# Running the 64-row products of a fused attention, gated and low-rank kernel over all 128 rows

## The chip, the cores and the metric

The kernel runs on one core of one Trainium2 chip. The metric is device time in microseconds (us) of the whole kernel. Engines: PE is TensorE's matrix products (PEld its weight loads), DVE is VectorE, ACT is ScalarE, POOL is GpSimd, SP is SyncE, which issues the transfers.

## What is computed

Three blocks follow each other: attention with rotary positions (4 batches, 8 heads, 576 tokens, 64 features per head), a gated block with a product over the tokens ("spatial mix"), and a block with a rank-32 product over the tokens followed by a two-layer channel block.

```
scores = (1/8) * q_rot @ k_rot.T;  attn = exp(scores - max) / (sum + 1e-9);  x = attn @ v      # per head
h = gelu(x @ w_in);  u, v = halves of h;  v_n = layernorm(v) * g_ln
x = x + (u * (w_sg @ v_n + b_sg)) @ w_out                   # w_sg is 576 x 576, over tokens
x = x + ((x.T @ U) @ V).T                                   # U is 576 x 32, V is 32 x 576
out = x + relu(x @ w_ch1) @ w_ch2
```

## The kernel before, in words

Products run in the type F32R (`float32r`), which keeps only part of a float32. To keep precision, an operand is split into a high part (a copy in that type) and a low part (what is left), and a product of two split operands is the sum of high x high, high x low and low x high. Tokens come in chunks of 128; 576 is four chunks and a tail of 64 (`TS`, L91). For a tail, one tile of 128 partitions holds the high part in its upper 64 partitions and the low part in its lower 64, so that one product over 128 rows does two of the three: the other operand then has its high part in both halves. The third product is the one that this change is about.

Attention (L119 to L465). The work runs in ticks, one for each chunk of a head's scores, 5 per head, 32 heads, in an order that is written out by hand on all engines (L424 to L458). In a tick `scores` makes one chunk of scores in PSUM (four products, L248), ScalarE takes the exponential, and for the first chunk and the tail (`SPLITS`, L136) it makes the high part `ph` (L257) and VectorE the low part (L263). `row_max` works ten chunks ahead: two products (L220) and VectorE's maximum (L225). Both use the three buffers "ss" of PSUM. `values`, three ticks behind, multiplies the probabilities with the values (L284) into two accumulators: an unsplit chunk takes four instructions in plain float32, the first chunk six products, and the tail, last, four. For the tail `VS` holds the high part of the values (index 0) and the low part (index 1); the 64 rows of the values stand twice in it, in both halves of the partitions. `finish` then copies the result to X (ACT, L299) and the sums of the exponentials to `sr` (DVE, L300); only after that may the next head's products into the two accumulators begin. Beside this, `later` puts steps at fixed ticks: rotary turns on POOL, and on ACT, DVE and POOL the conversion of one float64 chunk every ten ticks from tick 12 on (`converted`, with three longer DVE passes L74 to L76): eight chunks of w_in, one of U and two of V. Those of V write the high part `VH4` and the low part `VL2` (L352).

Gated block and low-rank product (L468 to L669). `v_step`, `u_step`, `s_step` (spatial mix), `o_step`, `y_step`, `z_step` and `h_step` (low-rank product with V) make products by `mm3` (L535), four PSUM tiles in turn; TensorE's order is written out (L753 to L843), that of the other engines is a scheduler's. `s_step` runs four times for each of 4 batches: twelve pairs of products for four chunks (L610), then the tail (L612) against the high part `WSH` and, over 64 rows, against the low part `WSL`. `h_step` runs four times per batch: `Z` holds its high part above and its low part below, against `VH4`, and then its upper half against `VL2`.

The channel block (L672 to L746) has no products of 64 rows.

The two lines for the tail of the probabilities and the low-rank product are:

```
280  pr = [(VS[:, 0, j], ph[:, ns]), (VS[:kk, 1, j], ph[:kk, ns])]      # kk = 64
668  mm3(ps, [(Z[:, ds_], VH4), (Z[0:64, ds_], VL2)], 2)
```

Of the kernel before, what the change touches and what calls it, by code (L numbers as in the profile page):

```python
# [17 lines left out]

# The high words of float64's 2**-127 and of the largest float32, read as float32.
F64_LEAST = 2.0**-15  # L20
# [5 lines left out]

# The chunks of keys whose probabilities are split for the product with the values.
SPLIT = slice(0, 5, 4)

# The attention runs in ticks, one for each tile of a head's scores. The other work is put between them:  # L30
# the steps that prepare a head's operands (three of rope, high parts, low parts, the row of -1), so many
# ticks before its first tile; for heads 2, 3 and 4, the ticks themselves; for heads 0 and 1, of the two
# steps of first_stacks.
LEAD = 23, 22, 19, 19, 15, 10
LEAD_IN = (-20, -19, -19, -8, -8, 1), (-19, -18, -16, -3, -1, 4), (-3, -3, 0, 2, 4, 8)
FIRST = (-17, -10), (-9, -9)
# The heads prepared without DMAs: which of their copies ScalarE makes.
BY_ACT = (0, 1, 1, 1, 1), (1, 1, 0, 1, 1), (1, 0, 1, 1, 1)
# Loads ahead of a head and of a pair's values, and the two steps of splitting the values.
LOAD, LOAD_FIRST, LOAD_V, SPLIT_V, SPLIT_V_FIRST = 30, -19, 16, (6, 1), (-11, -1)  # L40
# The maxima of rows: tiles ahead of the scores, the tick where that begins and its tiles in ten ticks,
# the tick for head 1's, and the ticks from a head's last tile of them until they are made a row.
AHEAD, RAMP_FROM, RAMP, MAX_1, ROW, ROW_0, ROW_1 = 10, -1, 25, -1, 2, -8, -9
# The steps of the sums' inverses, after a pair of heads.
INVERSE = 3, 4, 14
# The float64 matrices: first tick, ticks apart, ticks from load to arithmetic; and the split of the first rows.
MATRIX, APART, CONVERT, ROWS = 12, 10, 5, (151, 159)
# Idle products that keep TensorE's clock up until the pipeline is full: before the maxima of head 0, their
# row, the five tiles of maxima of head 1, and the first tiles of scores.
IDLE = 17, 2, 5, 0, 2, 5, 6, 1, 0, 1  # L50
# [3 lines left out]
def tile_kernel(ctx: ExitStack, tc: tile.TileContext, qk, vv, tabs, w_in, g_ln, wsgT, b_sg, w_out, u_r, v_r, w1, w2, out):  # L54
    nc = tc.nc

    def f(ap):
        return ap.bitcast(F32)
# [4 lines left out]
    def bits(ap):  # L63
        """The words of float64 rows, low and high by turns."""
        return ap.bitcast(U32)

    def from_f64(t, raw):
        """The steps of t = float32 of the float64 words in raw [p, n, 2]; too small a magnitude becomes 0."""
        lo, hi = raw[:, :, 0], raw[:, :, 1]
        tu = t.bitcast(U32)  # L70
        return (
            lambda: nc.scalar.activation(t, hi.bitcast(F32), AF.Abs),
            lambda: nc.vector.tensor_scalar(t, t, F64_LEAST, F64_MOST, ALU.max, ALU.min),  # L73
            lambda: nc.vector.tensor_scalar(tu, tu, 5, 2, ALU.logical_shift_left, ALU.logical_shift_right),  # L74
            lambda: nc.vector.scalar_tensor_tensor(tu, hi, 0xC0000000, tu, ALU.bitwise_and, ALU.bitwise_or),
            lambda: nc.vector.scalar_tensor_tensor(tu, lo, 29, tu, ALU.logical_shift_right, ALU.bitwise_or),  # L76
        )
# [21 lines left out]
    def staged(pool, src, tag="raw64", bufs=2):  # L99
        """float32 of the float64 words at src."""  # L100
        raw = pool.tile([P, 512, 2], U32, tag=tag, name=tag, bufs=bufs)
        t = pool.tile([P, 512], F32, tag="t64", name="t64", bufs=1 if tag == "raw64" else 2)
        nc.sync.dma_start(raw.rearrange("p n w -> p (n w)"), src)
        for fn in from_f64(t, raw):
            fn()
        return t

    keep = ctx.enter_context(tc.tile_pool(name="keep", bufs=1))
    # Halves of w_in, and later the first weights of the channel block.
    SETA = [keep.tile([P, KT, 512], F32R, name=f"setA{i}") for i in range(4)]  # L110
# [4 lines left out]
    VH4 = keep.tile([P, S], F32R, name="VH4")  # L115
    VL2 = keep.tile([64, S], F32R, name="VL2")

# [1 line left out]
    es1 = ExitStack()  # L119
# [28 lines left out]
    def rope(e, h):  # L148
        """The steps of turning a head's keys and queries, on engine e."""
        raw = RAW[h % NR]  # L150
        return (
            lambda: e.tensor_tensor(raw[:, 0], raw[:, 0], tab[:, 0], ALU.mult),
            lambda: e.tensor_tensor(raw[:, 1], raw[:, 1], tab[:, 1], ALU.mult),
            lambda: e.tensor_tensor(raw[:, 0], raw[:, 0], raw[:, 1], ALU.add),
        )

    def stacks(h, ticks):
        """Operands of the scores, of keys and queries in the halves of the partitions: K1 the
        keys' high parts twice, Q1 the queries' high and low parts, K2 the keys' low parts and -1,
        Q2 the queries' high parts and, later, the rows' maxima."""  # L160
        rot = RAW[h % NR][:, 0]
# [26 lines left out]
    def first_stacks(h):  # L188
        """The same without a wait for DMAs, in two parts."""
        rot = RAW[h % NR][:, 0]  # L190
# [23 lines left out]
    def row_max(h, t, done):  # L214
        """The maxima of a tile of head h's rows; and as a row, those that head `done` has."""
        ps = psp.tile([P, 2, 512], F32, tag="ss", name=f"sm{h}_{t}", bufs=3)
# [14 lines left out]
    def first_row():  # L231
        """Head 0's maxima as a row, without a DMA."""
        ps = psp.tile([P, 2, 512], F32, tag="ss", name="first_row", bufs=3)
# [31 lines left out]
    def values(h, c, t0):  # L265
# [4 lines left out]
        for n in range(2):  # L270
            ns = slice(n * HALF, (n + 1) * HALF)
            o = PVS[h][n][:, :HALF]
            if c in SPLITS:
# [3 lines left out]
                if kk == P:  # L277
                    pr = [(VS[:, 0, j], ph[:, ns]), (VS[:, 1, j], ph[:, ns]), (VS[:, 0, j], pl[:, ns])]
                else:
                    pr = [(VS[:, 0, j], ph[:, ns]), (VS[:kk, 1, j], ph[:kk, ns])]  # L280
            else:
# [41 lines left out]
    def converted(t0, src, n, use):  # L323
        """float32 of the n float64 columns at src, for the steps use(t)."""
        raw = p1.tile([P, 512, 2], U32, tag="raw64", name="raw64", bufs=1)[:, :n]
# [22 lines left out]
    def v_chunk(t0, a):  # L348
        hs = slice(a * HALF, (a + 1) * HALF)
        converted(t0, v_r[:, 2 * a * HALF:2 * (a + 1) * HALF], HALF, lambda t: (  # L350
            lambda: nc.scalar.activation(VH4[:, hs], t, AF.Copy),
            lambda: nc.gpsimd.tensor_tensor(VL2[:, hs], t[:D], f(VH4[:D, hs]), ALU.subtract),  # L352
        ))
# [59 lines left out]
    def warm(i):  # L413
        """Products of no use that keep the tensor engine's clock up."""
        if i == 0:
# [8 lines left out]
    for t in range(T0, NC * NH + LAG):  # L424
# [32 lines left out]
        for fn in due.pop(t, []):  # L457
            fn()  # L458
    # The last pair's last two steps come with the next block.
    while len(due) > 2:  # L460
# [6 lines left out]

# [1 line left out]
    es2 = ExitStack()  # L469
# [49 lines left out]
    def gelu2(dst, ps, w, pp):  # L519
        """2 * gelu_tanh(ps), in dst if there is one."""  # L520
        t = p2.tile([P, 2, 512], F32, tag="gt", name="gt", bufs=3)
# [24 lines left out]
    def x_tail(b):  # L546
        """The tails of the tokens of two batches."""
        for a in range(2):
# [7 lines left out]
    def v_step(b, t):  # L556
        """Normed rows of the tile t of tokens, at the end of a group of tiles; the tails of two batches are one tile."""
        if t == NC - 1 and b % 2:
# [46 lines left out]
    def s_step(b, d):  # L605
# [5 lines left out]
        tail = VT[:, ds_] if b % 2 else VH[:, NC - 1, ds_]  # L611
        pr += [(tail, WSH[:, NC - 1]), (tail[:D], WSL[:D, NC - 1])]  # L612
        mm3(ps, pr, 2)
# [19 lines left out]
    def y_step(b, s):  # L633
        """Rows of one or two tiles of tokens."""
        pp, nt = TS[s], min(2, NC - s)
# [28 lines left out]
    def h_step(b, d):  # L664
        Z = ZS[b]
        ps = ps_tile(f"q{b}_{d}")
        ds_ = slice(d * P, (d + 1) * P)
        mm3(ps, [(Z[:, ds_], VH4), (Z[0:64, ds_], VL2)], 2)
        nc.vector.tensor_tensor(h2(X[b][:, d]), ps[:, :, :HALF], h2(X[b][:, d]), ALU.add)  # L669

# [1 line left out]
    FG = 512  # L672
# [9 lines left out]
    def weights(pool, g, tiles):  # L682
        """The steps of loading a group's weights."""
        W[g] = tiles
# [7 lines left out]
    def spans(blk):  # L692
        """The pieces of a block of tokens that lie in one batch."""
        first = t = sum(WIDE[:blk])
# [15 lines left out]
    def c1(g, blk, i):  # L710
        """The hidden features of two tiles for a block of tokens."""
        if i == 0:
# [17 lines left out]
    def c2(g, blk, i, n=2):  # L730
        """The tiles n * i ... of output features for a block of tokens, of a group of hidden ones."""
        RH, RL = RS[g, blk]
# [14 lines left out]

# [1 line left out]
    def run(fn, b, *which):  # L749
# [153 lines left out]
```

## Time and profile before

| | us |
|---|---|
| median of 3 runs | 1003.77 |
| lowest, highest of the runs | 1003.36, 1005.98 |
| span of the profiled execution | 1002.3 |

The profiled execution's own time is given by its span, from its first to its last instruction. The page and the answers of the trace that follow are of that execution. PE is modelled: a product's busy time overlaps with its neighbours', so the pace of products is read from stretches of the chain (time by number of products) and not from a mean. In the chain, a line such as "PE pv L284 x8" stands for eight products in a row; "issue" is time in which an engine waited for nothing that the profile shows.

| stretch, us | what runs |
|---|---|
| 0 to 37 | loads, first head's operands |
| 37 to 335 | attention, 16 pairs of heads |
| 335 to 424 | gated block of batch 0 |
| 424 to 616 | low-rank product and gated block by turns, four batches |
| 616 to 1002 | channel block |

### The profile page before, as it was taken

The numbers are of one execution on the slowest core, as the hardware profiler recorded it, in microseconds if no ns is written. First come the engines' busy times: TensorE is split into PE (matmuls) and PEld (weight loads), VectorE is DVE, ScalarE is ACT, GpSimd is POOL, SyncE is SP. The second block draws the span as 40 slices with busy tenths as digits, with TensorE's granted clock in tenths as the row PEclk, the third lists the DMA queues.
The fourth block names the chain that finished last, engine by engine and source line by source line (L and its number), as shares of the span: only waits on it lengthen the run. The fifth ranks groups of instructions, "written<-read, shape, count | busy, mean of one in ns | idle before, by whom it ended". The sixth has DMA issues, their size and how long they took to land.

```text
span 1002.3 us, 13628 instructions
## 1 busy us (share of the span) xinstructions
PE 973.2 (97%) x5276; PEld 846.6 (84%) x5276; DVE 591.5 (59%) x856; ACT 390.6 (39%) x639; POOL 388.7 (39%) x340
## 2 busy tenths in 40 slices
PE   6899999999999998999999999999999999999998
PEld 2688878788888787989999888889988988899887
DVE  7778898888875488544744985554532452222222
ACT  4466666666666463422414451322211221101010
POOL 8668877787851474241422572221200120000000
PEclk8999999999999999999999999999999999999999
DMA  5567666766640400000000311231210110000112
GB/s 174 137 179 189 190 185 166 190 172 166 182 109 15 156 24 1 1 1 1 1 1 19 111 41 43 85 99 49 84 42 1 43 64 1 1 1 20 47 51 74
DMA packets 58967, 77.97 MB, mean 78 GB/s; under 512 B 30459, under 2 KB 34326, under 8 KB 58902
## 3 DMA queue, kind: packets, MB, share of 16 engines
q1 hardware_dynamic: 58902, 77.09, 26.6%
q8 instruction: 42, 0.69, 0.3%
q14 instruction: 23, 0.19, 0.1%
HBM read 55.02 MB, written 4.79 MB: 60 GB/s over the span
## 4 chain that ended last, share of the span: by engine, by line
PE 83%; DVE 10%; DMA 3%; issue 2%; POOL 1%; ACT 1%; SPq 0%; DVEq 0%; ACTq 0%; POOLq 0%
PE r L535 20%; PE a L535 20%; PE pv L284 13%; PE st L248 8%; PE sm L220 4%; PE u L535 4%; PE m L535 4%; PE w L535 4%; PE v L535 3%; DVE t L73 1%; DVE MX L225 1%; DMA g<-in_wsgT 1%; PE q L535 1%; DVE t L74 1%; DVE g L616 1%
## 5 line engine op out<-in xcount | busy, mean ns | idle before, releaser
L225 DVE TENSOR_REDUCE MX<-sm 128x1 f32<-128x576 f32 (+1 forms) x160 | 119.8, 752 | 28.4 <-PE sm L220 23.8
L248 PE MATMUL st<-Q,K 65*128 65x288 f32 (+3 forms) x640 | 126.6, 320 | 1.4 <-DVE ph L263 1.4
L727 ACT ACTIVATE RH<-r 128x944 fp32r<-128x944 f32 (+1 forms) x38 | 35.7, 940 | 212.0 <-PE r L535 211.9
L728 DVE SCALAR_TENSOR_TENSOR RL<-r,RH 128x944 fp32r<-128x944 f32 (+1 forms) x38 | 42.4, 1117 | 126.6 <-ACT RH L727 126.5
L284 PE MATMUL pv<-pc,VV 128*128 128x288 f32 x384 | 108.5, 406 | 0.0
L248 PEld LDWEIGHTS st<-Q,K 65*128 65x128 f32 (+3 forms) x640 | 94.2, 179 | 16.1 <-DVE ph L263 6.1
L743 DVE TENSOR_TENSOR X<-a,X 128x416 f32<-128x416 f32 (+4 forms) x65 | 46.4, 745 | 90.3 <-PE a L535 90.3
L535 PE MATMUL a<-RH,setB 128*128 128x472 f32 (+1 forms) x320 | 95.6, 371 | 0.0
L535 PE MATMUL a<-RH,setA 128*128 128x472 f32 (+1 forms) x288 | 86.1, 370 | 0.0
L220 PE MATMUL sm<-K,Q 128*128 128x288 f32 (+1 forms) x320 | 72.6, 311 | 13.6 <-ACT Q L196 6.0
L535 PE MATMUL r<-UH,setA 128*128 128x472 f32 (+1 forms) x256 | 77.4, 375 | 0.0
L284 PEld LDWEIGHTS pv<-pc,VV 128*128 128x128 f32 x384 | 66.7, 190 | 11.7
L535 PE MATMUL r<-UH,setB 128*128 128x472 f32 (+1 forms) x256 | 76.4, 369 | 0.0
L284 PE MATMUL pv<-ph,VS 128*128 128x288 f32 (+1 forms) x256 | 74.6, 362 | 0.6 <-DVE sr L300 0.3
L251 ACT ACTIVATE pc<-st 128x576 f32<-128x576 f32 x96 | 62.2, 649 | 31.8 <-PE st L248 30.8
L494 POOL TENSOR_TENSOR setB<-t,setB 128x512 fp32r<-128x512 f32 x16 | 20.7, 1293 | 127.0 <-ACT setB L688 63.0
L220 PEld LDWEIGHTS sm<-K,Q 128*128 128x128 f32 (+1 forms) x320 | 50.1, 182 | 20.8 <-DVE MX L225 10.1
L535 PEld LDWEIGHTS a<-RH,setB 128*128 128x128 f32 x320 | 60.2, 188 | 6.9
L284 PEld LDWEIGHTS pv<-ph,VS 128*128 128x128 f32 (+1 forms) x256 | 44.1, 187 | 21.1 <-issue 8.4
L535 PE MATMUL a<-RL,setB 128*128 128x472 f32 (+1 forms) x160 | 59.6, 372 | 0.0
L535 PEld LDWEIGHTS a<-RH,setA 128*128 128x128 f32 x288 | 54.1, 188 | 6.1
L255 ACT ACTIVATE st<-st 128x576 f32<-128x576 f32 x64 | 40.2, 628 | 42.8 <-PE st L248 37.6
(180 smaller groups left out, 2219.3 us busy)
## 6 DMA issues: line engine op xcount, KB each, us to landing
raw<-in_qk SPq DMA_DIRECT2D x31, 576.0 KB
Q<-K SPq DMA_DIRECT2D x87, 144.0 KB
raw<-in_w SPq DMA_DIRECT2D x24, 512.0 KB
VV<-in_vv SPq DMA_DIRECT2D x32, 160.0 KB
rb<-rr SPq DMA_DIRECT2D x30, 144.0 KB
K<-K SPq DMA_DIRECT2D x29, 144.0 KB
raw<-in_w_in SPq DMA_DIRECT2D x8, 512.0 KB
gt<-in_w SPq DMA_DIRECT2D x8, 512.0 KB
```

Of the source, the lines that this page charges most:

```text
L73: lambda: nc.vector.tensor_scalar(t, t, F64_LEAST, F64_MOST, ALU.max, ALU.min),
L220: nc.tensor.matmul(ps[:TS[t], n, :HALF], Q1[:, t * P:t * P + TS[t]], K1[:, n * HALF:(n + 1) * HALF], start=True, stop=True)
L225: nc.vector.tensor_reduce(MXs[h % 2][:TS[t], t:t + 1], ps[:TS[t], :, :HALF], AX.XY, ALU.max)
L248: nc.tensor.matmul(ps[:kk, n, :HALF], l[:, c * P:c * P + kk], r[:, ns], start=st, stop=not st)
L251: nc.scalar.activation(h2(pc[:kk]), ps[:kk, :, :HALF], AF.Exp, scale=0.125)
L255: nc.scalar.activation(pc, pc, AF.Exp, scale=0.125)
L284: nc.tensor.matmul(o, l, r, start=(c == 0 and j == 0), stop=(c == NC - 1 and j == len(pr) - 1))
L494: return nc.gpsimd.tensor_tensor(out, a, b, ALU.subtract)
L535: nc.tensor.matmul(o, l, rr, start=(j == 0), stop=(j == n - 1))
L727: nc.scalar.activation(RH[:, s], ps[:, :, :WIDE[blk]], AF.Relu)
L728: nc.vector.scalar_tensor_tensor(RL[:, s], ps[:, :, :WIDE[blk]], 0.0, f(RH[:, s]), ALU.max, ALU.subtract)
L743: nc.vector.tensor_tensor(X[b][:, e2, xs], ps[:, :n, us], X[b][:, e2, xs], ALU.add)
```

## The change

The three products over 64 rows now run over all 128 rows. In the lower half they multiply the low part of the one operand with the low part of the other, a term that was left out before. For that the low part of V, which was only on 64 partitions, is computed for all 128 (`VL4`); `VS` and `WSL` had both halves already, and `TS` and every order are as they were. Each engine issues the same instructions in the same sequence with the same waits as before.

```diff
-    VL2 = keep.tile([64, S], F32R, name="VL2")
+    VL4 = keep.tile([P, S], F32R, name="VL4")
...
-                    pr = [(VS[:, 0, j], ph[:, ns]), (VS[:kk, 1, j], ph[:kk, ns])]
+                    pr = [(VS[:, 0, j], ph[:, ns]), (VS[:, 1, j], ph[:, ns])]
...
-            lambda: nc.gpsimd.tensor_tensor(VL2[:, hs], t[:D], f(VH4[:D, hs]), ALU.subtract),
+            lambda: nc.gpsimd.tensor_tensor(VL4[:, hs], t, f(VH4[:, hs]), ALU.subtract),
...
-        pr += [(tail, WSH[:, NC - 1]), (tail[:D], WSL[:D, NC - 1])]
+        pr += [(tail, WSH[:, NC - 1]), (tail, WSL[:, NC - 1])]
...
-        mm3(ps, [(Z[:, ds_], VH4), (Z[0:64, ds_], VL2)], 2)
+        mm3(ps, [(Z[:, ds_], VH4), (Z[:, ds_], VL4)], 2)
```

The two instructions that it alters besides the products stand on POOL, in the second half of the attention. The names end in the tile's number; `t` is the converted chunk of V.

```order
 L153 TENSOR_TENSOR raw_93<-raw_93,tab 128x576
-L352 TENSOR_TENSOR VL_81<-t_180,VH_80 64x288
+L352 TENSOR_TENSOR VL_81<-t_180,VH_80 128x288
 L186 TENSOR_TENSOR VS_123<-VV_119,VS_123 128x2x64
```

Nothing moves there; the subtraction covers 128 partitions instead of 64. (PE's list shows no row of difference, since it gives a product's output, 128 x 288, which is the same.)

## Rows read from the trace of the kernel before

**Rows 1.** The page: busy shares, TensorE's slices, and shares of the chain.
```profile
PE 973.2 (97%) x5276; PEld 846.6 (84%) x5276; DVE 591.5 (59%) x856; ACT 390.6 (39%) x639; POOL 388.7 (39%) x340
...
PEclk8999999999999999999999999999999999999999
...
PE 83%; DVE 10%; DMA 3%; issue 2%; POOL 1%; ACT 1%; SPq 0%; DVEq 0%; ACTq 0%; POOLq 0%
```

**Rows 2.** TensorE's groups by shape: rows*columns, input, count | busy us, mean ns.
```profile
L248 PE MATMUL st<-Q,K 65*128 65x288 f32 x256 | 54.8, 295 | 0.0
L284 PE MATMUL pv<-ph,VS 64*128 64x288 f32 x64 | 25.3, 395 | 0.0
L535 PE MATMUL q<-VL,Z 64*128 64x288 f32 x32 | 8.4, 343 | 0.0
...
L284 PEld LDWEIGHTS pv<-ph,VS 128*128 128x128 f32 (+1 forms) x256 | 44.1, 187 | 21.1 <-issue 8.4
```

**Rows 3.** The chain in order of time, 287 to 310: start us, us, what.
```profile
290.98 2.08 PE pv L284 x8
293.06 0.73 PE st L248 x4
...
294.59 0.80 PE pv L284 x6
...
296.46 0.97 PE pv L284 x4
```

**Rows 4.** The chain in order of time, 318 to 640, the second block's products.
```profile
425.14 1.64 PE q L535 x8
426.78 3.38 PE u L535 x24
...
495.53 16.16 PE m L535 x112
```

**Rows 5.** POOL's groups by line, 80 to 300: count | busy us, mean ns | idle before.
```profile
L336 POOL TENSOR_TENSOR setA<-t,setA 128x512 fp32r<-128x512 f32 x7 | 9.1, 1294 | 27.4 <-ACT setA L335 27.4
L352 POOL TENSOR_TENSOR VL<-t,VH 64x288 fp32r<-64x288 f32 x2 | 1.6, 800 | 7.1 <-ACT VH L351 7.1
L344 POOL TENSOR_TENSOR U<-t,U 128x160 fp32r<-128x160 f32 x2 | 1.1, 526 | 3.6 <-ACT U L343 3.6
```

**Rows 6.** Two pairs of heads: length, busy PE, PEld, DVE, ACT, POOL, PEclk, DMA, GB/s.
```profile
138.53:157.76 19.23, 19.05 (x107) 15.60 (x107) 16.83 (x27) 13.03 (x25) 15.23 (x14) 1.00 0.68 184
290.98:309.20 18.22, 18.22 (x107) 15.58 (x107) 13.52 (x23) 11.60 (x22) 3.83 (x5) 1.00 0.21 51
```

**Rows 7.** Timelines of DVE (141.6 to 153) and PE (149 to 153): start us, us, what.
```profile
143.24 0.76 DVE L225 TENSOR_REDUCE MX<-sm 128x1 f32<-128x576 f32 x1 [0.84 <-PE sm L220]
...
147.74 1.70 DVE L75 SCALAR_TENSOR_TENSOR t<-raw,t 128x512 uint32<-128x512 uint32 x1
...
151.49 0.80 DVE L300 TENSOR_SCALAR sr<-pv 1x288 f32<-1x288 f32 x2
...
151.99 0.53 PE L284 MATMUL pv<-ph,VS 128*128 128x288 f32 x2
```

**Rows 8.** The chain in order of time, where it leaves TensorE in the second block.
```profile
394.18 11.64 PE w L535 x74
...
552.29 0.82 DVE g L615
...
587.12 0.68 DVE X L669
```

**Rows 9.** The chain in order of time, at the start of the channel block.
```profile
612.94 3.48 PE q L535 x16
616.42 17.19 PE r L535 x72
633.61 5.13 PE a L535 x24
```

**Rows 10.** The same columns for a stretch behind 616.
```profile
616.60:620.02 3.42, 3.42 (x10) 2.86 (x10) 0.62 (x1) 2.77 (x3) 1.95 (x2) 0.50 0.51 158
```

## The prediction

> **What bounds the kernel now.** I read the page's busy shares and its chain of waits first [rows 1]. TensorE is busy for 97% of the span of 1002.3 us, and 83% of the chain that ended last runs through it; VectorE holds 10% of that chain. So time saved on TensorE is, at first sight, time saved, except where the chain leaves TensorE. The groups by shape come next [rows 2]: they show which products have 64 rows. There are 64 of them over the tails of the probabilities and 32 in the low-rank product, and a further 32 in the spatial mix (two groups of 16, not shown), 128 in all, and every one reads its left and right operand from partitions 0 to 63. Products of 65 rows stand beside them at the 295 ns of any product.
>
> What such a product costs is not its own mean (busy times of pipelined matmuls overlap) but the pace of the chain, which is where I looked next, in two heads of the attention that wait for nothing [rows 3]. Six products of 288 columns take 0.80 us, so 0.133 each; the four instructions of a chunk that is not split take 0.97. The stretch "pv x8" is such a chunk (0.97) and then the four products of the tail: 2.08 - 0.97 = 1.11 us, where four at 0.133 would take 0.53. The four score products behind it take 0.73, which is 0.20 more than four at that pace. So one head's tail loses 0.58 + 0.20 = 0.78 us. In program order the tail's products have 128, 64, 128, 64 rows, and 128 follow: four changes of the row count, **0.195 us each**.
>
> The block after the attention says the same in another order [rows 4]. A step of the low-rank product has two products of 128 rows and two of 64, so two changes. Two steps ("q x8") take 1.64 us instead of 8 x 0.133 = 1.06, and the 24 products behind take 3.38 instead of 24 x 0.133 = 3.19: 0.77 for four changes, 0.39 for a step. The spatial mix has the same two changes in a step: 112 products (four steps) take 16.16 instead of 14.90, 1.26 more, and part of the last change falls into what follows. I use 0.39 a step for both.
>
> **The change, part by part.** It alters no order: every engine issues the same instructions in the same sequence with the same waits, and only the partition ranges of 128 products and of two GpSimd instructions grow.
>
> *The products.* A product of 128 rows and 288 columns runs at 0.133 [rows 3]; the changed ones become that form, between neighbours of that form. So every change of the row count goes, and nothing is paid for the added rows. TensorE sheds 32 heads x 0.78 = 25.0 us in the attention, and 16 + 16 steps x 0.39 = 12.5 us behind it. The products wait for nothing new: the first product of each tail already reads all 128 partitions of its operands, and the added halves come from instructions that write all 128. What counts is how much of the 37.5 us stands on the path.
>
> *The low part of V.* GpSimd subtracts over 128 partitions instead of 64, twice. Its time goes by columns: 160 columns over 128 partitions take 526 ns, 512 take 1294 [rows 5], so 288 come to some 805 by a straight line, and the 64-partition form now takes 800. It costs nothing. If it did cost double, 2 x 0.8 us would lie in GpSimd's 7.1 us of idle time before these two.
>
> *Attention, pairs with a converted matrix.* Of the 16 pairs of heads, eight convert one 512-column chunk of w_in each (ticks 12 to 82, one per ten ticks). Such a pair lasts 19.23 us and keeps VectorE busy for 16.83 of them; a pair without conversions lasts 18.22 [rows 6]. Without the switches TensorE would need 18.22 - 1.56 = 16.66 for a pair, less than VectorE's 16.83, so here the saving can't all arrive. Where it stops is seen in one pair [rows 7]. VectorE waits 0.84 us for TensorE's maxima before 143.24, and the first head's saving of 0.78 fits in that: the whole burst that begins there moves up by 0.78. But from there on it works without a break, with the passes of a conversion between its other work (the longest 1.70), and the second head's tail lies inside. At the end of the burst stand the two sums (L300, 0.80 for two, from 151.49) that free the accumulators of the next head, and TensorE's next products into them start at 151.99. TensorE may come there 1.56 earlier; the sums come 0.78 earlier. So I take **0.78 per pair**, 8 x 0.78 = 6.2 us. The bounds: nothing at all (VectorE as it is sets 19.23) and the full 1.56.
>
> *The other pairs.* Three pairs convert a smaller chunk (U, and V in halves). Their bounds are the same, 0.78 and 1.56; I take the middle, 1.2, since the passes are shorter: 3.6 us. Five pairs convert nothing. There VectorE has 13.52 us of work in 18.22 [rows 6], so the saving is whole: 5 x 1.56 = 7.8. The attention gives 17.6 us, between 10 and 25.
>
> *Gated block and low-rank product.* Eleven of the 32 steps lie where the chain runs on VectorE or GpSimd, and I look at these by batch [rows 8]. The four spatial steps of batch 0, before 382, stand beside VectorE's g and conversion passes, which carry the chain until GpSimd releases TensorE at 394.18: no gain. For batch 3 the chain leaves TensorE after the first spatial step, at 552.29, and comes back at 587.84, past the residual add of the low-rank product of batch 2 at 587.12: three spatial and four low-rank steps there gain nothing. That leaves 32 - 4 - 3 - 4 = 21 steps on the chain: 21 x 0.39 = 8.2 us. The bounds are 12.5 (all) and about 6 (only the 16 steps between 424 and 512).
>
> *The clock.* From 616.60 to 620.02 the granted clock is 0.50, the 1.2 GHz level, and right before it stand the four low-rank steps of batch 3, 16 products in 3.48 us [rows 9, 10]. The 72 products behind take 17.19 us instead of 72 x 0.214 = 15.4 (24 take 5.13): 1.8 us lost. TensorE was not waiting there, it ran through eight changes of the row count, with a product every 0.22 us instead of 0.133. Without them I expect this fall to go, **1.8 us**; against it speaks that the same steps of batch 2, which end at 587 [rows 8], were followed by no fall, so the lower bound is 0.
>
> *Sum.* 6.2 + 3.6 + 7.8 + 8.2 + 1.8 = 27.6 us. The profiled execution would go from a span of 1002.3 to 974.7. The median of the runs, 1003.8, lies 1.5 us over that span (what lies around it, and the spread of the runs); the same difference gives **976.2 us**.
>
> **The rivals.**
>
> *All of it arrives.* 37.5 us, and 1.8 for the clock: 964.5. For it: TensorE's 97%. It needs VectorE's burst to give way in the eight pairs, and the eleven hidden steps to lie on the path after all. Against it: VectorE's 16.83 us in a pair of 16.66, and the chain at 361 to 394 and 552 to 588. Chance 0.12.
>
> *VectorE takes more.* If the pairs with conversions keep their 19.23 us, because the sums (L300) stand behind the conversion in the first head too, the attention gives 11.4, and with 8.2 and an unchanged clock the total is 19.6: 984.2. For it: 16.83 us of work besides waits whose cause may not move, such as the DMA that carries the sums. Against it: the 0.84 us in which VectorE waits for TensorE. Chance 0.16.
>
> *The change doesn't do what it says.* The extra 0.195 us could come from exposed weight loads instead of the row count, and would then stay at 128 rows: 1003.8. A load lasts 187 ns and a product of 288 columns follows every 133 [rows 2, 3], so loads of 128 rows are hidden behind products of 128 rows everywhere else, and the six-product stretch alternates between two stationary operands as the tail does. Chance 0.03. The Trainium skill (TensorE: Matmul & The Clock Gate, Part 3, "What overlaps and what doesn't") states that a weight load overlaps running products only when its row group differs. By that rule a load of rows 0 to 127 would wait for any product, each product would cost load plus stream before and after, and this rival would be the forecast; the trace disagrees, since the load alone lasts longer than the 133 ns at which the products follow each other.
>
> *Slower.* Products over full rows could make the clock fall more often. At the half level the stretch at 616.60 lost 1.8 us. To lose the forecast's 25.8 us (without the clock term) takes more than fourteen further falls like that; slower by 3 us takes sixteen. For it: the clock does fall in this trace. Against it: in the stretch from 620 to 1002, where all products have 128 rows, PEclk is 9 tenths or more in every slice [rows 1]. Chance 0.02.
>
> **How the numbers follow.** The forecast has the rest, 0.67, with 970 to 982 for its own range. The range 966 to 985 takes in the case in which VectorE takes more (984.2) and all but the top of the case in which all arrives (964.5 with the clock term, 966.3 without). About 0.3%, 3 us, is what a measurement of this kernel can tell from no change. Faster by more: 0.67 + 0.12 + 0.16 = 0.95; same 0.03; slower 0.02.
>
> **What the changed profile should show.** No product of 64 rows is left. In the chain "pv x8" falls from 2.08 to 1.50 and the scores behind it from 0.73 to 0.53; "q x8" from 1.64 to 1.06. A pair without conversions lasts 16.7 us, one with a w_in chunk 18.4, and TensorE waits there for the sums of L300. TensorE waits longer in 361 to 394 and 552 to 588 (as counted now), whose lengths hold. The fall of the clock behind the last low-rank step is gone. The prediction is wrong if products of 128 rows in these places still start more than 0.2 us apart, if pairs with conversions keep 19.2 us, or if these pairs too come down to 17.7.

## The result, and the profile after

| | before | after |
|---|---|---|
| median, us | 1003.57 | 988.09 |
| lowest, highest of 4 runs | 1002.88, 1005.98 | 985.88, 988.67 |
| span of the profiled execution | 1002.3 | 986.9 |

The ratio is 0.9838, with an interval of 0.9821 to 0.9855: the kernel became faster by 1.6%, some 15.5 us. The forecast was 27.6 us, so the direction is right and the time, 988.1 instead of 976.2, lies above the range. The question is where 12 us of the expected gain went.

The page first, with the lines that answer to [rows 1]:

```profile
PE 944.8 (96%) x5275; PEld 843.2 (85%) x5276; DVE 594.9 (60%) x856; ACT 387.8 (39%) x639; POOL 388.7 (39%) x340
...
PEclk7899999999999998999999999999999999999999
...
PE 77%; DVE 15%; DMA 2%; issue 2%; POOL 1%; ACT 1%; SPq 0%; DVEq 0%; ACTq 0%; POOLq 0%
```

TensorE has lost 28.4 us of busy time (973.2 to 944.8) and the span only 15.4. Its share of the chain has gone from 83% to 77%, VectorE's from 10% to 15%: part of what TensorE shed has become waiting for VectorE. The chain in order of time, from 284 to 290, answers to [rows 3]:

```profile
284.15 1.49 PE pv L284 x8
285.65 0.54 PE st L248 x4
...
286.98 0.79 PE pv L284 x6
...
288.84 0.97 PE pv L284 x4
```

Here everything came as forecast: "pv x8" from 2.08 to 1.49, the scores behind it from 0.73 to 0.54, together 0.78 us for a head. Two windows answer to [rows 6], with the same columns; the first is a pair of heads with a chunk of w_in, the second a pair without:

```profile
135.58:154.63 19.05, 17.94 (x109) 15.35 (x106) 17.23 (x28) 12.92 (x25) 15.36 (x14) 1.00 0.69 188
283.88:300.57 16.69, 16.69 (x108) 15.34 (x106) 13.27 (x23) 11.38 (x22) 3.67 (x5) 1.00 0.23 56
```

The pair without conversions went from 18.22 to 16.69 (forecast 16.66). The pair with a chunk of w_in went from 19.23 to 19.05 (forecast 18.45); TensorE is busy for 17.94 of it, and VectorE's busy time has risen from 16.83 to 17.23 although it has the same instructions. Behind the attention, again from the chain in order of time, as [rows 4, 9]:

```profile
416.73 1.06 PE q L535 x8
417.79 3.19 PE u L535 x24
...
478.89 0.77 DVE X L669
...
483.17 14.80 PE m L535 x112
...
574.01 6.97 PE r L535 x24
...
600.65 2.12 PE q L535 x16
602.78 15.46 PE r L535 x72
```

Low-rank and spatial steps have the pace of products of 128 rows, with a new wait for VectorE at 478.89. The 72 products of the channel block take 15.46 instead of 17.19, so the fall of the clock at 616 is gone; but the 24 products at 574.01 take 6.97, and the same products took 5.40 in the kernel before:

```profile
587.84 5.40 PE r L535 x24
```

The window of the kernel after there shows a granted clock of 0.50, the 1.2 GHz level (PEclk, behind the busy times of the five engines):

```profile
574.31:577.70 3.39, 3.39 (x10) 2.85 (x9) 3.39 (x3) 0.63 (x1) 3.39 (x2) 0.50 0.00 0
```

Setting the start of the same instruction in both traces side by side gives the account, term by term, against the forecast's sum:

| us gained | forecast | measured |
|---|---|---|
| five pairs without conversions | 7.8 | 6.6 |
| eight pairs with a chunk of w_in | 6.2 | 3.4 |
| three pairs with U or V | 3.6 | 1.1 |
| begin of the gated block (334 to 394) | 0 | -1.6 |
| 16 steps between 424 and 512, one spatial and four low-rank steps later | 8.2 | 6.8 |
| clock, all falls from 28 us on | 1.8 | -0.9 |
| sum | 27.6 | 15.4 |

Pairs are counted here from one first head's "pv x8" to the next one's. The largest miss, 5.3 us, is in the eleven pairs with conversions, and the experiments are mostly about these.

**What holds such a pair.** VectorE's timeline in the pair from 135.58 (start us, us, what) answers to [rows 7]:

```profile
139.78 0.76 DVE L225 TENSOR_REDUCE MX<-sm 128x1 f32<-128x576 f32 x1 [0.40 <-PE sm L220]
140.46 1.40 DVE L73 TENSOR_SCALAR t<-t 128x512 f32<-128x512 f32 x1
...
142.44 0.96 DVE L74 TENSOR_SCALAR t<-t 128x512 uint32<-128x512 uint32 x1
...
144.89 1.70 DVE L75 SCALAR_TENSOR_TENSOR t<-raw,t 128x512 uint32<-128x512 uint32 x1
...
148.05 0.67 DVE L76 SCALAR_TENSOR_TENSOR t<-raw,t 128x512 uint32<-128x512 uint32 x1
148.65 0.80 DVE L300 TENSOR_SCALAR sr<-pv 1x288 f32<-1x288 f32 x2
```

GpSimd's timeline in the same stretch:

```profile
140.16 1.41 POOL L171 TENSOR_TENSOR K<-raw,K 128x576 fp32r<-128x576 f32 x1
141.53 1.59 POOL L154 TENSOR_TENSOR raw<-raw 128x576 f32<-128x576 f32 x1
...
144.63 1.42 POOL L153 TENSOR_TENSOR raw<-raw,tab 128x576 f32<-128x576 f32 x1
149.46 1.29 POOL L336 TENSOR_TENSOR setA<-t,setA 128x512 fp32r<-128x512 f32 x1 [3.41 <-ACT setA L335]
```

The same two views of the kernel before, VectorE and then GpSimd:

```profile
143.92 0.77 DVE L73 TENSOR_SCALAR t<-t 128x512 f32<-128x512 f32 x1
...
145.27 0.98 DVE L74 TENSOR_SCALAR t<-t 128x512 uint32<-128x512 uint32 x1
```

```profile
142.99 1.41 POOL L171 TENSOR_TENSOR K<-raw,K 128x576 fp32r<-128x576 f32 x1
144.36 1.60 POOL L154 TENSOR_TENSOR raw<-raw 128x576 f32<-128x576 f32 x1
...
147.48 1.41 POOL L153 TENSOR_TENSOR raw<-raw,tab 128x576 f32<-128x576 f32 x1
152.61 1.29 POOL L336 TENSOR_TENSOR setA<-t,setA 128x512 fp32r<-128x512 f32 x1 [3.72 <-ACT setA L335]
```

Read the ends. After, L73 ends at 141.86, and GpSimd's L171 at 141.57: 0.29 earlier. Before, 144.69 and 144.40: 0.29 again. L74 ends 0.28 to 0.29 us behind L154, and L75 0.54 to 0.55 behind L153, in both kernels. Counted from the first head's "pv x8" (138.53 before, 135.85 after), VectorE's burst (MX) begins 0.78 us earlier, as forecast; but L171 comes only 0.15 earlier, L73 ends only 0.15 earlier, and the sums (L300) come 0.16 earlier. TensorE's next products start at 149.14, behind the sums, as forecast, but 0.6 us later than forecast. L73 has become longer by 0.63, which isn't work: it is a wait for GpSimd that stands inside the instruction's duration.

GpSimd in turn waits 3.41 us (before 3.72) for ScalarE's L335, which needs L76's result. So the two go in a circle: GpSimd's row of work for two heads, L75's end behind its last rotary instruction, then pl, MX, mt, L76, L335, and GpSimd again. GpSimd's busy time and its wait fill the pair: 15.36 + 3.41 = 18.8 of 19.05 after, 15.23 + 3.72 = 18.95 of 19.23 before. TensorE isn't in that sum. This is the theory that the experiments put to test: that VectorE's passes wait for GpSimd (the lock theory of the expectations), and that this wait and GpSimd's wait for L335 form a circle (the loop theory).

### The profile page after: what moved, and what is told of

Its sections match the earlier page's. It is cut to its first block, busy times and chain, and to the rows that moved or that the text cites. A ratio compares the mean times of both kernels' runs of the same rounds, so it can differ in the third digit from the quotient of the medians.

```text
span 986.9 us, 13627 instructions
## 1 busy us (share of the span) xinstructions
PE 944.8 (96%) x5275; PEld 843.2 (85%) x5276; DVE 594.9 (60%) x856; ACT 387.8 (39%) x639; POOL 388.7 (39%) x340
## 3 DMA queue, kind: packets, MB, share of 16 engines
q1 hardware_dynamic: 58902, 77.09, 27.6%
## 4 chain that ended last, share of the span: by engine, by line
PE 77%; DVE 15%; DMA 2%; issue 2%; POOL 1%; ACT 1%; SPq 0%; DVEq 0%; ACTq 0%; POOLq 0%
PE r L535 20%; PE a L535 20%; PE pv L284 10%; PE st L248 6%; PE u L535 4%; PE w L535 4%; PE m L535 4%; PE sm L220 3%; PE v L535 3%; DVE MX L225 2%; DVE t L75 2%; DVE t L73 2%; DVE t L76 1%; DVE t L74 1%; DVE ph L263 1%
## 5 line engine op out<-in xcount | busy, mean ns | idle before, releaser
L220 PE MATMUL sm<-K,Q 128*128 128x288 f32 (+1 forms) x320 | 73.3, 314 | 16.7 <-DVE MX L225 9.1
L535 PEld LDWEIGHTS a<-RH,setA 128*128 128x128 f32 x288 | 54.1, 188 | 6.1
L284 PE MATMUL pv<-ph,VS 128*128 128x288 f32 x256 | 56.4, 325 | 2.7 <-DVE sr L300 1.5
L73 DVE TENSOR_SCALAR t<-t 128x512 f32<-128x512 f32 (+2 forms) x47 | 35.3, 751 | 31.9 <-ACT t L72 31.5
```

The source lines that it names most:

```text
L220: nc.tensor.matmul(ps[:TS[t], n, :HALF], Q1[:, t * P:t * P + TS[t]], K1[:, n * HALF:(n + 1) * HALF], start=True, stop=True)
L284: nc.tensor.matmul(o, l, r, start=(c == 0 and j == 0), stop=(c == NC - 1 and j == len(pr) - 1))
L535: nc.tensor.matmul(o, l, rr, start=(j == 0), stop=(j == n - 1))
```

## The experiments

Times are medians; the kernel before ran beside them with 1003.9 to 1005.5.

**Each part alone.** `tails_only` changes line 280 only, `mix_lowrank_only` the rest (with `VL4` in place of `VL2`).

```diff
-                    pr = [(VS[:, 0, j], ph[:, ns]), (VS[:kk, 1, j], ph[:kk, ns])]
+                    pr = [(VS[:, 0, j], ph[:, ns]), (VS[:, 1, j], ph[:, ns])]
```

```diff
-        pr += [(tail, WSH[:, NC - 1]), (tail[:D], WSL[:D, NC - 1])]
+        pr += [(tail, WSH[:, NC - 1]), (tail, WSL[:, NC - 1])]
...
-        mm3(ps, [(Z[:, ds_], VH4), (Z[0:64, ds_], VL2)], 2)
+        mm3(ps, [(Z[:, ds_], VH4), (Z[:, ds_], VL4)], 2)
```

> Only the tails of the probabilities run over 128 rows (line 280); the spatial mix and the low-rank product are as before. In the trace of the changed kernel TensorE stood 10.4 us earlier at the end of the attention and 8.4 us earlier at 405 us. If parts simply add, this kernel keeps about 8 to 9 us of gain: 994 to 996 us. If the rest of the change is what made the attention's gain small (it shares no resource with it that I see), more than 12 us, below 992.

> Only the spatial mix and the low-rank product run over 128 rows; the attention is as before. Additive theory: 5.5 us between 405 and 512, 1.4 in the last four low-rank steps and up to 1.7 from the fall of the clock behind them, some of it given back by a fall elsewhere: 995 to 998 us. Prediction's sum (21 steps on the path and the clock): 10 us, 993.6.

Measured: 994.71 (994.54 to 995.18), ratio 0.9903 with 0.9877 to 0.9929; and 996.12 (995.74 to 996.92), 0.9917 with 0.9895 to 0.9939. Both are in their expected ranges. The product of the ratios, 0.9821, is the lower end of the whole change's interval (0.9821 to 0.9855): within what the runs can tell, the parts add up. `tails_only` also decides on the clock. It keeps the switches in the low-rank steps; its chain:

```profile
604.89 3.48 PE q L535 x16
608.38 15.62 PE r L535 x72
```

The same sixteen products in the same 3.48 us as in [rows 9], and the 72 behind them run at the full pace. So the switches alone weren't what made the clock fall there. `before_norope` (below) shows the same, 15.62 behind 3.48, and has the fall at the other place, 24 products in 6.95 at 569.49, with the switches in place.

**The price of a change of the row count.** `before_tail_grouped` is the kernel before with the tail's products in the order 128, 128, 64, 64 rows: two changes instead of four, and no more rows.

```diff
-                nc.tensor.matmul(o, l, r, start=(c == 0 and j == 0), stop=(c == NC - 1 and j == len(pr) - 1))
+                if c < NC - 1 or j == 0:
+                    nc.tensor.matmul(o, l, r, start=(c == 0 and j == 0), stop=(c == NC - 1 and j == len(pr) - 1))
+        if c == NC - 1:
+            for n in range(2):
+                nc.tensor.matmul(PVS[h][n][:, :HALF], VS[:kk, 1, SPLITS.index(c)], ph[:kk, n * HALF:(n + 1) * HALF], start=False, stop=True)
```

> The kernel before with the tail's four products in the order 128, 128, 64, 64 rows: still two products of 64 rows, two changes of the row count instead of four. If the price is one of a change (0.195 us), a tail costs 0.39 less, a pair without conversions 17.45 instead of 18.22, and the attention gains 4 to 6 us: 998 to 1000.5 us. If each product of 64 rows has a price of its own, nothing changes: 1002 to 1006 us.

Measured: 998.16 (996.32 to 1001.62, 6 runs), ratio 0.9934 with 0.9904 to 0.9963; a pair without conversions lasts 17.40. Its chain (L288 is the line of the two products of 64 rows):

```profile
277.16 1.23 PE pv L285 x6
278.39 0.46 PE pv L288 x2
278.84 0.72 PE st L248 x4
```

A chunk of 0.97 and two products of 0.13 make 1.23, so nothing is lost among equal rows; the two of 64 rows lose 0.19, and the scores behind them 0.19. Two changes, 0.195 each, as worked out from [rows 3]; half of the 1.54 for a pair is 0.78, and 18.22 - 0.78 = 17.44. The Trainium skill (TensorEngine Tiling (Array Packing), Key Properties) states that a change of the tiling mode drains TensorE, without a time for it; these traces agree, and the time is 0.195 us here. Products of 65 rows beside those of 128 pay nothing: four score products, two of each kind, take 0.54 in the kernel after (285.65), which is four times 0.133.

**Who holds the pairs with conversions.** `after_norope` leaves out GpSimd's three rotary instructions of every head from head 5 on, `after_nopasses` VectorE's passes L73 to L76 for the chunks that are converted in the attention; `before_norope` and `before_nopasses` do the same to the kernel before.

```diff
-            steps = rope(nc.gpsimd, h) + (high, low, lambda: nc.gpsimd.memset(f(K2[D:D + 1]), -1.0))
+            steps = (lambda: None,) * 3 + (high, low, lambda: nc.gpsimd.memset(f(K2[D:D + 1]), -1.0))
```

```diff
-            later(t0 + CONVERT + j, fn)
+            if not 1 <= j <= 4:
+                later(t0 + CONVERT + j, fn)
```

> The changed kernel without GpSimd's three rotary instructions per head (L152 to L154) from head 5 on; the scores of these heads are then those of unturned keys and queries, and the same number of products, maxima and exponentials. VectorE's instructions are all as they were. Lock theory: VectorE's passes of a conversion (L73, L74, L75) wait for the end of the GpSimd instruction that runs when they start, some 2.6 us in a pair; with GpSimd mostly idle they last 0.3 to 0.7 us each and a pair with a conversion falls from 19.0 to 16.7 to 17.5 us, the kernel to 970 to 977 us. Rival (the amount of VectorE's work, as predicted): its work proper is unchanged, the pair stays above 18.5, the kernel at 984 to 989 us.

> The changed kernel without VectorE's four passes (L73 to L76) over the chunks converted in the attention, so that w_in, U and V are wrong numbers of another size; loads, ScalarE's and GpSimd's steps stay. It sizes all that the passes cost with the tail's products at full pace. Both theories: the pair falls to TensorE's 16.7 to 17.0 us, eight pairs by 2.0 and three by 1.5, the kernel to 966 to 971 us. If it stays above 18, neither holds, and the transfers or GpSimd set the pair.

> The kernel before with GpSimd's three rotary instructions of a head left out from head 5 on, as in after_norope (958.7 us): the scores of those heads are of unturned keys and queries. The two kernels differ by the change alone. Lock theory (VectorE's conversion passes wait for GpSimd's instructions, and this holds the pairs with conversions): with GpSimd's rows gone all pairs are TensorE's, 18.2 us here against 16.7 there, so the change is worth about 1.4 a pair x 16 = 22 to 25 us in the attention and the 5 to 6 that it gave behind it, 27 to 31 together: 986 to 990. Rival (VectorE's own amount of work, or the conversions by some other wait, hold the pairs with conversions): the change is worth what it was worth with the rotary work, 15 to 17: 973 to 976.

> The kernel before with VectorE's passes L73 to L76 left out for the chunks converted within the attention, as in after_nopasses (968.2 us): the weights w_in, U and V hold what was in the tiles. Lock theory: without the passes every pair here is TensorE's 18.2 us (19.2 before), against 16.7 to 17.0 in after_nopasses; the change is then worth 1.4 a pair, 20 to 23 us in the attention, and 5 to 6 behind it, 25 to 29 together: 993 to 997. Rival (the pairs are held by GpSimd's row of work alone, waits of ScalarE or transfers): a pair stays near 19 and the time at 1000 to 1004.

| us | before | after | worth of the change |
|---|---|---|---|
| as it is | 1003.57 | 988.09 | 15.5 |
| no rotary work on GpSimd | 985.44 (984.24 to 987.95) | 958.68 (956.53 to 958.91) | 26.8 |
| no passes on VectorE | 994.42 (992.71 to 994.63) | 968.21 (966.51 to 971.07) | 26.2 |

Take away GpSimd's rotary work or VectorE's passes, and the change is worth 11 us more. (Each kernel of a row ran beside the kernel before, which differed by 0.8 us between the two occasions; that is small beside 11.) VectorE's passes in `after_norope`:

```profile
124.67 0.42 DVE L73 TENSOR_SCALAR t<-t 128x512 f32<-128x512 f32 x1
...
125.67 0.41 DVE L74 TENSOR_SCALAR t<-t 128x512 uint32<-128x512 uint32 x1
...
127.57 0.68 DVE L75 SCALAR_TENSOR_TENSOR t<-raw,t 128x512 uint32<-128x512 uint32 x1
...
129.69 0.67 DVE L76 SCALAR_TENSOR_TENSOR t<-raw,t 128x512 uint32<-128x512 uint32 x1
```

The same four instructions take 2.18 us; in the kernel after they take 4.73, and in the kernel before 0.77 + 0.98 + 1.70 [rows 7] + 0.67. Windows of a pair with a chunk of w_in, in `before_norope` and then in `after_norope`:

```profile
114.50:132.73 18.23, 18.23 (x109) 15.61 (x107) 15.05 (x27) 13.03 (x25) 6.09 (x7) 1.00 0.73 193
```

```profile
125.38:142.08 16.70, 16.70 (x109) 15.35 (x107) 14.69 (x27) 12.81 (x25) 6.11 (x7) 1.00 0.79 213
```

VectorE still does every pass, and TensorE is busy throughout. In `before_norope` all fourteen pairs between the first and the last take 18.22 to 18.23; in `after_norope` they take 16.66 to 17.7. The rival, that VectorE's own amount of work holds them, falls: it asked for 984 to 989 with GpSimd idle, and for a worth of 15 to 17 in the pair of kernels. GpSimd's row of work alone doesn't hold them either: `after_nopasses` keeps it, and eight of its eleven pairs that had conversions last 16.7 to 17.0. The lock theory's sizes were not exact either. `after_norope` came out 11 us below its lower end, of which 7 are at the start of the kernel, which also lost rotary work (the first scores start at 25.3 instead of 32.7 us); `before_norope` came out half a microsecond below its range. The two without passes are in theirs.

**One pass fewer.** `after_noclamp` leaves out L73 for the chunks that are converted in the attention.

```diff
-            later(t0 + CONVERT + j, fn)
+            if j != 1:
+                later(t0 + CONVERT + j, fn)
```

> The changed kernel without the clamp L73 of each converted chunk in the attention (magnitudes beyond float32's range would come out differently; these inputs have none). It takes 1.40 us of VectorE in a pair and sits ahead of L74. Lock theory: of the 1.40 only 0.3 is work, the next pass takes over most of the wait, since it too ends after a GpSimd instruction, and the last ones (L75) still end with L153: the pair falls by 0.1 to 0.5, the kernel to 983 to 988 us. Rival (VectorE's busy time counts as work): the pair falls by 1.0 to 1.4, the kernel to 976 to 980 us.

Measured: 977.12 (974.88 to 977.64), ratio 0.9711 with 0.9679 to 0.9743, and five of the eight pairs with a chunk of w_in last 17.4 to 17.6. The time is the one that the rival had asked for, and below the lock theory's. The two timelines suggest why, VectorE and then GpSimd:

```profile
138.88 1.71 DVE L75 SCALAR_TENSOR_TENSOR t<-raw,t 128x512 uint32<-128x512 uint32 x1
```

```profile
138.63 1.41 POOL L152 TENSOR_TENSOR raw<-raw,tab 128x576 f32<-128x576 f32 x1
```

L75 still takes 1.7 us, so the pass is no cheaper and still waits; but it now ends 0.55 behind L152, no longer behind L153, which comes next. In these five pairs L74 and L75 each end behind the GpSimd instruction before the one they waited for, L74 behind L171 and L75 behind L152, and a pair is shorter by about the length of one of these, 1.4 us. Work of 0.4 us (L73 without a wait) was worth 1.5 in such a pair: 11 us in all. This reading was found after the run; no further run tests it.

**The way back to GpSimd later.** In `after_low_later` and `before_low_later` GpSimd's step behind a conversion (L336, L352) comes three ticks later, so that it need not wait for L76; `after_noclamp_later` adds this to the run above.

```diff
-            later(t0 + CONVERT + j, fn)
+            later(t0 + CONVERT + j + (3 if j == 6 and n > 160 else 0), fn)
```

> The changed kernel, with GpSimd's low part of a converted chunk (L336 and L352) three ticks later, behind its next rotary work, so that GpSimd does not stand 3.4 us in front of it. Loop theory: pairs of heads with a conversion last 19.0 us because VectorE's passes over SBUF (L73, L74, L75) end 0.28 to 0.55 us after a GpSimd instruction, their last pass releases ScalarE, that releases L336, and L336 stands before GpSimd's next rotary work: with L336 later the loop is open and a pair falls to 17.5 to 18.4 us, the kernel to 975 to 983 us. Rival, the prediction's: the amount of VectorE's work and the place of the sums (L300) set the pair; then it stays at 19.0 and the kernel within 985 to 991 us.

> The kernel before with the same delay of L336 and L352 and nothing else. Loop theory: the loop set the 19.24 us of such a pair before the change already, so the pair falls to TensorE's 18.3 to 18.6 and the kernel to 995 to 999 us. Rival (TensorE set the pair before, with the stalls of VectorE's burst): no change, 1001 to 1006 us.

> The changed kernel without the clamp L73 of the chunks converted in the attention and with L336 and L352 three ticks later. If the two gains measured apart (11 us and 2.5 us) come from different waits they add: 973 to 976 us. If both only shorten the same loop of GpSimd and VectorE, the second adds nothing: 976 to 980 us.

Measured: 985.61 (982.48 to 987.21), 1005.74 (1003.58 to 1008.14, 10 runs; ratio 1.0008 with 0.9994 to 1.0023) and 976.18 (974.55 to 979.08). The first two are misses of the loop theory, which expected 975 to 983 and 995 to 999, and lie in the ranges of its rivals (985 to 991 and 1001 to 1006). The third lies where the two expected ranges meet, and its runs fall on both sides of 976, so it doesn't tell whether the gains add. GpSimd's wait for L335 did go, but another came in its place. The longest wait of GpSimd between 66 and 300, in the kernel after and then in `after_low_later` (us, times, longest):

```profile
POOL setA L336 <- ACT setA L335: 28.2, 8, 4.3
```

```profile
POOL K L177 <- DMA Q<-K: 34.9, 17, 3.6
```

GpSimd is early at its next step, waits there for a transfer that copies the queries' low parts out of the tile it is to write, and meets the passes again: in the pairs around 105 and 122 L73 takes 0.67 and 1.29, L74 0.97 and 0.96, and most pairs last 18.0 to 19.0. The wait has moved to another pass. `before_low_later`, VectorE and then GpSimd:

```profile
109.22 0.68 DVE L75 SCALAR_TENSOR_TENSOR t<-raw,t 128x512 uint32<-128x512 uint32 x1
...
111.34 1.37 DVE L76 SCALAR_TENSOR_TENSOR t<-raw,t 128x512 uint32<-128x512 uint32 x1
```

```profile
110.76 1.41 POOL L171 TENSOR_TENSOR K<-raw,K 128x576 fp32r<-128x576 f32 x1 [1.89 <-ACT K L166]
```

L75 no longer waits, but L76, which took 0.67 in the kernel before, ends 0.54 behind L171. Over the eight chunks of w_in the four passes take 3.8 us a chunk here and 4.0 in the kernel before, 4.3 in `after_low_later` and 4.5 in the kernel after. So opening the circle at this one place hardly shortens the passes' waits, and that the circle sets the length of a pair is argued, not shown. Whether the moved wait is the whole reason why the kernel before gains nothing stays open. None of these versions is shown to beat the kernel after while computing all that it computes: the ranges of 985.61 and 988.09 overlap.

**GpSimd busy, but not reading.** In `after_memset` each rotary instruction is a memset that writes 1152 elements of bf16.

```diff
-            steps = rope(nc.gpsimd, h) + (high, low, lambda: nc.gpsimd.memset(f(K2[D:D + 1]), -1.0))
+            steps = (lambda: nc.gpsimd.memset(RAW[h % NR][:, 1].bitcast(BF16), 0.0),) * 3 + (high, low, lambda: nc.gpsimd.memset(f(K2[D:D + 1]), -1.0))
```

> The changed kernel with each of GpSimd's three rotary instructions per head, from head 5 on, replaced by a memset of 1152 bf16 columns on the unused half of the same tile: GpSimd stays occupied, but these instructions read nothing; the scores are those of unturned keys and queries. If VectorE's passes wait because GpSimd reads SBUF while they run, L75 falls from 1.70 to about 0.7 us and the pair with a conversion to 16.7 to 17.6 us, the kernel to 958 to 972 us, near the kernel without the rotary work. If it is GpSimd's occupation as such (its row of instructions and its wait for L335 as a loop), the pair stays above 18.3 and the kernel at 980 to 988 us.

Measured: 976.59 (975.48 to 976.99), ratio 0.9723 with 0.9701 to 0.9745, in neither theory's range, with the start shortened as in `after_norope`. A pair lasts 18.62. GpSimd, then VectorE:

```profile
130.15 3.33 POOL L177 MEMSET raw<- 128x1152 bf16 x3
```

```profile
130.37 2.12 DVE L73 TENSOR_SCALAR t<-t 128x512 f32<-128x512 f32 x1
...
133.07 0.69 DVE L74 TENSOR_SCALAR t<-t 128x512 uint32<-128x512 uint32 x1
135.25 0.68 DVE L75 SCALAR_TENSOR_TENSOR t<-raw,t 128x512 uint32<-128x512 uint32 x1
```

GpSimd's three memsets end at 133.48, and L74 ends at 133.76, 0.28 behind them; L73 waited through two of them and ended 0.28 behind the second. So a pass with one input waits for a GpSimd instruction that only writes, too. L75 met no GpSimd instruction here, so this run says nothing on passes with two inputs.

## Why the prediction was wrong, point by point

**What a change of the row count costs** was right: 0.195 us in the chain, in a kernel with half the changes, and in every "pv" and "q" of the kernel after. That weight loads are what costs, the rival with 1003.8, is refuted by the same lines. The spatial mix gave a little less, 16.16 to 14.80, so 0.34 a step where the forecast took 0.39.

**Pairs without conversions** were right: 16.69 against 16.66. But the last pair of the attention gave 0.5 instead of 1.56, for there the chain leaves TensorE for VectorE and a transfer (rb, 3.05 us at 328.53 before, 3.24 at 318.63 after), which the prediction didn't count: 6.6 of 7.8 us. Right too were GpSimd's two subtractions over 128 partitions, which take 804 ns each where 805 were forecast, and cost nothing.

**Pairs with a chunk of w_in**: this is the step that failed. The prediction said that "the whole burst that begins there moves up by 0.78", since VectorE waits 0.84 us for the maxima. The burst did begin 0.78 earlier, counted from the first head's "pv x8". But its end, the sums, moved by 0.16 only, since its passes end at GpSimd's instructions, which came 0.15 earlier. The prediction counted 16.83 us of VectorE's busy time as work and named no GpSimd. Of L73's 0.77, L74's 0.98 and L75's 1.70 us, some 0.35, 0.57 and 1.0 were waiting, by the 0.42, 0.41 and 0.68 that they take with GpSimd idle. Of 0.78 a pair, six of the eight pairs were left with 0.0 to 0.35; the first and the seventh gained 1.3 and 1.1: 3.4 us of 6.2. For most of these pairs the lower bound, "nothing at all", was nearly the truth, and the prediction's own sign of being wrong, pairs that keep 19.2 us, came close (19.05). The rival "VectorE takes more" (984.2, chance 0.16) came nearest in time, though the waits it had in mind, such as that for a transfer, weren't the ones.

**Pairs with U or V** took the middle between two bounds that both rested on the same step: 1.1 us instead of 3.6.

**What VectorE and GpSimd do once the gated block begins earlier** was set at nothing, and the two traces differ there by 1.6 us. VectorE's L509 before, after, and GpSimd after:

```profile
344.26 0.46 DVE L509 TENSOR_SCALAR bh<-bh 128x576 f32<-128x576 f32 x1 [1.71 <-DMA bh<-in_b_sg]
```

```profile
334.56 1.55 DVE L509 TENSOR_SCALAR bh<-bh 128x576 f32<-128x576 f32 x1
```

```profile
334.35 1.45 POOL L494 TENSOR_TENSOR WSL<-g,WSH 128x576 fp32r<-128x576 f32 x1 [3.21 <-ACT WSH L504]
```

L509 now starts inside a GpSimd subtraction, ends 0.31 behind it and takes 1.1 us longer, and the chain of the kernel after runs through it. That the change causes this isn't shown. L509 takes 0.46 to 1.63 us in the traces of the fourteen kernels, 1.03 in `mix_lowrank_only`, whose attention is as before; and the time from the block's first product to the first one with w_out is 52.8 to 54.5 us in them: 52.9 in the kernel before, 54.1 in the kernel after, and longest in `before_nopasses`, where L509 takes 0.46.

**The steps behind the attention** gave 6.8 us of 8.2. The eleven hidden steps gave nothing, as forecast; the kernel after is 13.9 us ahead at 548 (time before) and 13.8 at 588. Part of the rest, 0.4 us, went into a new wait for VectorE's L669 at 478.89.

**The clock** was wrong in its mechanism. The fall behind the last low-rank step did go, and the 72 products gained 1.7 us; but `tails_only` and `before_norope` keep the switches and have no fall there either (15.62 us for the 72 products in both). In the kernel after, a fall came at 574, where the 24 products lost 1.6 us. Two earlier falls lasted longer in the kernel after: one at 383 (6.8 us instead of 3.4 at 394), behind which 74 products take 11.97 instead of 11.64 [rows 8], and one at the start, where the granted clock is 0.50 until 35.0 us instead of 32.9 and the first product into the accumulators comes 0.75 later. The term came to -0.9 instead of 1.8. What sets where a fall comes isn't settled, and no such term should have been counted.

So the forecast's 27.6 us became 15.4 by 2.8 (w_in) + 2.5 (U, V) + 1.2 (pairs without conversions) + 1.6 (gated block) + 1.4 (steps) + 2.7 (clock) = 12.2 us. The step that failed accounts for 5.3 of these; the clock and the gated block differ between traces of kernels without any tie to this change, so the miss there may be chance in part.

## What to carry to other kernels

Between matrix products, look at changes of the row count before counting rows: 64 rows among 128 cost 0.195 us at each change, padding them with useful terms takes that away, and grouping them halved it here. Before you count another engine's busy time as work, compare one instruction's durations across the trace: where it ends again and again at a fixed distance behind an instruction of another engine, its duration holds a wait, and what comes earlier in front of it only waits longer. Where two engines wait for each other, a gain on a third engine can be lost in their waits, and removing one wait may only move it to the next instruction, as the later low parts did here.

## What the runs showed of the hardware that wasn't expected

VectorE's passes over SBUF wait for a running GpSimd instruction, inside their own duration, and at 512 columns end 0.28 us behind it with one input and 0.55 with two: L73 takes 0.42 us with GpSimd idle, 1.40 beside a rotary instruction, and 2.12 through two memsets. The distance goes with the columns of the pass: it is 0.10 and 0.19 at 160 columns, and 0.17 and 0.32 at 288, so hardly any of a pass seems to be done before GpSimd's instruction ends. GpSimd pays too, with the instruction in which such a pass ends: L154 takes 1.59 instead of 1.41 where L73 ends in it. The Trainium skill (SBUF — State Buffer, SBUF: two separate sides) states that VectorE and GpSimd share one pair of ports as an exclusive lock, held for a whole instruction while the other engine blocks; on VectorE's side it names instructions in a mode that uses both ports, and those with two SBUF inputs, the latter only against a GpSimd instruction that reads. The traces agree: passes with one input wait for a rotary instruction and for a memset alike, and those with two for a rotary instruction. In which mode the passes ran no run here shows.
